# Three heads of k and w_phi's second copy on other DMA queues, zero matmuls in a bank of their own, and a new order

## The chip, the cores and the metric

The kernel runs on one core of a Trainium2 chip. The metric is the device time of one execution in microseconds (us), as the median of the runs. The engines are TensorE (PE, with its weight loads as PEld), VectorE (DVE), ScalarE (ACT), GpSimd (POOL) and SyncE (SP). SP issues DMAs only; ACT and POOL can issue them too. In this kernel POOL's loads cast fp32 to bf16 on the way; those of SP and ACT do not cast.

## The reference

Linear attention with a Hedgehog feature map over 8 batches, 8 heads, 576 positions and 64 dimensions, followed by a gated feed-forward network (FFN) on 4608 tokens:

```python
def phi(x):
    proj = np.einsum('bhsd,df->bhsf', x, w_phi)
    proj = proj - np.max(np.abs(proj), axis=-1, keepdims=True)
    return np.concatenate([np.exp(proj), np.exp(-proj)], axis=-1)
q_p, k_p = (phi(q), phi(k))
kv = np.einsum('bhsf,bhsd->bhfd', k_p, v)
z = np.sum(k_p, axis=2)
num = np.einsum('bhsf,bhfd->bhsd', q_p, kv)
den = np.einsum('bhsf,bhf->bhs', q_p, z)[..., None] + 1e-06
attn = num / den
...
x = attn.transpose(0, 2, 1, 3).reshape(B * S, H * D)
out = (np.maximum(x @ w_gate, 0.0) * (x @ w_val)) @ w_out
```

w_phi is 64 x 128, w_gate and w_val are 512 x 1536, w_out is 1536 x 512; all inputs are fp32.

## The kernel before

The whole program is one list of steps, ORDER, written out in full. Each word is one step: a two-letter name, its arguments, the PSUM banks after a colon, and after an @ the buffer of a ring that it takes. A loop at the end runs through the list and calls `do_<name>`, so ORDER sets the order of the instructions on every engine and every DMA queue; each engine runs its own steps in that order, and waits for semaphores in it.

Each batch goes through the same stages, and the FFN of earlier batches is laid between them:

- **Loads.** `lk`, `lq`, `lm`, `ln` (k, q and the last 64 positions of each) are cast to bf16 by POOL's queue, and so are the weights `wl` (w_val, w_gate) and `wo`. `lv` and `lw` (v) go over SP's queue, except for batch 0, where `lv` goes over POOL's. HEADS splits the eight heads into groups 0 (two heads), 1 and 2 (three each). `wp` and `wq` load two copies of w_phi over SP's queue: w32f, read four times into 32 rows, and w64f, read twice into 64 rows; `wc` and `wd` cast them to bf16 on DVE. `gt` is a small DMA on SP that reads k's group 0 of batch 0 and so holds SP's queue until that group has landed.
- **k of batch 0** (`k0`, `k1`, `k2`): PE transposes a group's k into a bank (`k0`), DVE copies it to kT (`k1`), and PE multiplies it by w64 into four banks (`k2`). The other batches transpose on DVE (`kt`, `ku`) and project with `kr`, which uses w32.
- **k's features**: `ke` are the exponentials on ACT (two signs for each of four banks), `kx` the row maxima of the magnitudes on DVE, `kk` and `kp` the exponentials of these maxima. `vs`, `vd`, `vr`, `vo`, `vp` scale v by them, on POOL and DVE.
- **q's features**: `qt` transposes on DVE, `qs` and `qc` project on PE with w32, `qe` are the exponentials on ACT, `qx` the maxima on DVE; `qy`, `qz`, `qu`, `qw` turn these into scales.
- **kv and the numerators**: `kv` on PE, copied out by `kc` (ACT) or `kd` (DVE); `nu` on PE, joined on DVE by `nt`, `nv` and `nr`, divided on POOL by `nx`.
- **FFN**: `xp`, `xa` and `xc` (or `xt`, a DMA) transpose the result, `pv`, `pg`, `fv`, `fg` project it, `va`, `vb`, `pa`, `pb`, `pc`, `ga` are copies and products on ACT and DVE, `fo` and `fp` the output projection, `oc` and `oe` its copies, `od` the store. `mt`, `mc`, `me`, `mx`, `mn` and others do the same for the last 64 positions of q.

`zz.N` are N matmuls of a zeroed tile into a bank that nobody reads; `zero` is filled by `ms.0`, and `ms` steps fill other constants. At the start PE's queue holds zz.37, k0.1, zz.5, k2.1, zz.6, k0.2, zz.7, k2.2, k0.0, zz.7, k2.0, then the eight `qs` of batch 0, `qy` and the three `kv`.

Of the kernel before, what the change touches and what calls it, by code (L numbers as in the profile page):

```python
# [34 lines left out]
nt.0.1.1:1@t2 qz.0.3:4@my0 nu.0.1.2:5 qw.0.2 nv.0.1.1:1@u1 lq.1.2 nt.0.1.2:5@t0 kr.1.1:7630
nx.0.0@xu0 ke.1.1.3.1:0@kp2 wl.1.1 ke.1.1.0.0:7 nu.0.1.0:2 nt.0.1.0:2@t2 nu.0.2.0:4 xp.0.0:1
xa.0.0:1 nv.0.1.2:5 nv.0.1.0:2 wo.0 nu.0.2.1:5 nr.0.1@r0 nx.0.1@xu0 kx.1.1.3:0@mk2 wl.0.2 nu.0.2.2:2
lm.2.0 nt.0.2.1:5@t2 ke.1.1.3.0:0 nt.0.2.2:2@t0 nt.0.2.0:4@t1 ke.1.1.1.1:6 lm.2.1 qu.0.3@mz0
kx.1.1.2:3 pv.1.0:1 pa.1.0:1@val0 ke.1.1.1.0:6 nv.0.2.0:4@u1 nv.0.2.1:5 nv.0.2.2:2 nr.0.2@r0
pg.0.0:0 nx.0.2@xu1 kx.1.1.0:7 kx.1.1.1:6 qw.0.3 xp.0.1:1 nu.0.3.1:4 xa.0.1:1 ke.1.1.0.1:7  # L40
ke.1.1.2.0:3 nt.0.3.1:4@t0 nv.0.3.1:4@u0 qt.1.1@qT0 pv.0.0:5 pa.0.0:5@val1 pv.0.1:1 pb.0.0:0
pg.0.1:7 kk.1.1.0@ek1 pa.0.1:1@val2 ke.1.1.2.1:3 lw.1.0 xp.0.2:5 xa.0.2:5 qc.1.1:1462
qe.1.1.3.1:2@qp2 qe.1.1.2.1:6@qp0 qe.1.1.0.0:1@qp1 pb.0.1:7 lv.1.3 lv.1.1 qx.1.1.1:4 qe.1.1.2.0:6
qe.1.1.0.1:1 nu.0.3.2:0 nt.0.3.2:0@t0 kt.1.0 nu.0.3.0:5 nv.0.3.2:0 nt.0.3.0:5@t2 pv.1.1:3
pa.1.1:3@val2 qe.1.1.1.1:4@qp3 qx.1.1.2:6 qx.1.1.0:1 kk.1.1.1 vo.1.1@vs2 qx.1.1.3:2 pv.0.2:7
nv.0.3.0:5 pa.0.2:7@val1 qe.1.1.3.0:2 pg.1.1:0 pb.1.1:0 nr.0.3@r0 ln.0.0 pg.0.2:6 pb.0.2:6 pg.1.0:1
qe.1.1.1.0:4 kr.1.0:2573 ke.1.0.1.1:5@kp0 ke.1.0.3.1:3 ke.1.0.2.1:7 ke.1.0.0.0:2 ke.1.0.3.0:3
pv.1.2:4 qt.1.0@qT0 kx.1.0.1:5@mk2 lw.1.1 pa.1.2:4@val1 ke.1.0.0.1:2 nx.0.3@xu1 xp.0.3:6 xc.0.3:6
kx.1.0.2:7 wl.1.2 pg.1.2:0 pb.1.0:1 ke.1.0.2.0:7 ke.1.0.1.0:5 kx.1.0.3:3 pv.0.3:6 pa.0.3:6@val0
fv.0.8:4 va.0.8:4@val2 ln.0.1 qc.1.0:5371 wo.2 pv.1.3:6 vs.1.1.0 kx.1.0.0:2 kk.1.0.0@ek0 kk.1.0.1  # L50
qe.1.0.1.1:3 vr.1.0.1 vs.1.0.0@vs0 pb.1.2:0 qx.1.0.2:7 qx.1.0.0:5 kt.1.2@kT1 qe.1.0.2.1:7
qe.1.0.3.0:1 qe.1.0.0.0:5 vr.1.1.0 qe.1.0.2.0:7 ms.1 pc.1.3:6@val1 pg.0.3:4 pb.0.3:4 qx.1.0.3:1
fv.0.10:0 va.0.10:0@val3 fv.0.11:2 lk.2.3 qe.1.0.0.1:5 va.0.11:2@val0 qx.1.0.1:3 kr.1.2:0476
kx.1.2.0:0@mk2 ke.1.2.3.0:6@kp1 pg.1.3:5 fg.0.11:2 kx.1.2.2:7 kx.1.2.3:6 qe.1.0.1.0:3 ke.1.2.1.1:4
kx.1.2.1:4 ke.1.2.2.0:7 qe.1.0.3.1:1 ku.2@kT1 ke.1.2.0.1:0 pb.1.3:5 kk.1.2.0@ek2 ke.1.2.2.1:7
fv.0.9:3 va.0.9:3@val1 fg.0.8:1 ke.1.2.1.0:4 wo.1 lv.2.3 ga.0.11:2 vr.1.0.0 qy.1.0:7 qz.1.0:7@my0
mt.0 fg.0.10:5 ga.0.8:1 kk.1.2.1 ke.1.2.0.0:0 vs.1.0.1 mc.0:4732 me.0.2.0:3 mx.0.3:2 me.0.0.0:4
qu.1.0@mz0 mx.0.2:3 me.0.0.1:4 vr.1.1.1 vo.1.0 kv.1.0:0 kc.1.0:0@kv1 ga.0.10:5 mx.0.0:4 qw.1.0@cq0
mx.0.1:7 vs.1.1.1 kv.1.1:1 me.0.2.1:3 kc.1.1:1 nu.1.1.0:0 nt.1.1.0:0@t2 fg.0.9:5 vo.1.2@vs1 lv.2.0
kt.2.1@kT0 vs.1.2.1 nu.1.0.0:1 me.0.3.1:2 ga.0.9:5 ke.1.2.3.1:6 nu.1.0.1:4 nu.1.1.1:3 nt.1.1.1:3@t0  # L60
nt.1.0.0:1@t1 vs.1.2.0 kv.1.2:6 nv.1.1.0:0@u0 nv.1.1.1:3 me.0.1.0:7 kt.2.0 lw.2.1 fo.0.1.0:5
kc.1.2:6 nu.1.0.2:6 nt.1.0.2:6@t0 nu.1.1.2:3 nt.1.0.1:4@t2 me.0.3.0:2 nu.1.2.0:2 nt.1.2.0:2@t3
nv.1.0.0:1@u1 me.0.1.1:7 lq.2.2 nv.1.0.2:6 nv.1.0.1:4 nr.1.0@r0 nv.1.2.0:2@u2 fo.0.1.1:5 fo.0.1.2:5
oc.0.1:5@ob0 nt.1.1.2:3@t2 nu.1.2.2:4 nt.1.2.2:4@t3 lw.2.0 nv.1.1.2:3 nr.1.1@r1 kr.2.0:2617
ke.2.0.0.0:2@kp0 kx.2.0.3:7@mk2 lv.2.1 ke.2.0.0.1:2 od.0.1 nu.1.2.1:0 nt.1.2.1:0@t2 nx.1.0@xu1
kx.2.0.2:1 ke.2.0.1.1:6 kx.2.0.0:2 nu.1.3.2:5 nt.1.3.2:5@t0 nv.1.2.1:0 ke.2.0.3.1:7 fo.0.0.0:3
fo.0.0.1:3 nv.1.3.2:5@u1 xt.1.0 fo.0.0.2:3 nu.1.3.0:5 ke.2.0.2.1:1 nv.1.2.2:4 nr.1.2@r0
nt.1.3.0:5@t3 nx.1.1@xu0 nu.1.3.1:0 nt.1.3.1:0@t0 nv.1.3.0:5 nv.1.3.1:0 nr.1.3@r1 ke.2.0.3.0:7
ke.2.0.2.0:1 oc.0.0:3@ob0 ke.2.0.1.0:6 kt.2.2@kT1 nx.1.2@xu2 kr.2.1:4172 ke.2.1.2.0:7@kp1 kx.2.0.1:6
fo.0.2.0:3 fo.0.2.1:3 ke.2.1.1.1:1 xt.1.1 ke.2.1.0.1:4 ke.2.1.3.1:2 fo.0.3.0:0 ke.2.1.0.0:4  # L70
# [996 lines left out]
```

## Time and profile before

| what | value |
|---|---|
| time, median of 3 runs | 378.46 us (378.4 to 378.5) |
| the profiled execution | 378.79 us, span 376.8 us |
| mean granted TensorE clock in it | 0.986 |
| PE busy | 367.3 us (97%) |
| DVE busy | 296.3 us (79%) |
| ACT busy | 222.6 us (59%) |
| POOL busy | 161.4 us (43%) |
| chain that ended last | PE 89%, DVE 5%, ACT 4%, DMA 2% |
| DMA | 38.04 MB in 90513 packets |

The page cuts the span into 40 slices of 9.4 us and prints a digit for the busy share of each (9 is 90% or more); PEclk is the clock that PE was granted, in tenths of full speed. The chain of waits goes back from the last instruction, at each step to what released it, and gives start, length and what. Windows give busy time in chosen stretches, with the number of instructions, the clock, the DMA share and the bytes moved. PE's busy time is that of pipelined matmuls with modelled ends, so PE can be busy without doing its best.

### The profile page before, as it was taken

To read this page: it belongs to the slowest core of one execution; us is meant where nothing else is said; L and a number is where in the kernel's file an instruction comes from. 1 tells how busy PE (TensorE), PEld (TensorE's weight loads), DVE (VectorE), ACT (ScalarE), POOL (GpSimd) and SP (SyncE) were. 2 spreads that over 40 slices of the span, in tenths; PEclk is the share of its full clock that TensorE was granted. 3 is DMA by queue.
4 is the path that set the end of the run, shared out by engine and by line. 5 is a ranking of instruction groups with operands and counts; after the bars stand their busy time and mean duration, and the time that the engine had idled before them with its cause. 6 is when DMAs were issued, how large, how long until landed. Compare 5 with 4: busy or idle time off the path is not lost.

```text
span 376.8 us, 9181 instructions
## 1 busy us (share of the span) xinstructions
PE 367.3 (97%) x3591; PEld 197.2 (52%) x3591; DVE 296.3 (79%) x680; ACT 222.6 (59%) x539; POOL 161.4 (43%) x180
## 2 busy tenths in 40 slices
PE   8788999999999999999999999999999999999996
...
PEclk9859999999999999999999999999999999999999
...
DMA packets 90513, 38.04 MB, mean 101 GB/s; under 512 B 64230, under 2 KB 85734, under 8 KB 90470
## 3 DMA queue, kind: packets, MB, share of 16 engines
...
q10 hardware_dynamic: 144, 0.13, 0.1%
...
## 4 chain that ended last, share of the span: by engine, by line
PE 89%; DVE 5%; ACT 4%; DMA 2%; issue 0%; SPq 0%; DVEq 0%; ACTq 0%
PE bank L916 46%; PE bank L977 22%; PE bank L658 6%; PE bank L757 4%; PE bank L945 4%; PE bank L694 3%; ACT kp L563 2%; PE bank L511 2%; DMA w64f<-in_w_phi_dram 2%; DVE mk L571 1%; ACT qp L709 1%; PE bank L1006 1%; PE bank L898 1%; DVE u L788 1%; DVE maxq L717 1%; DVE t L778 1%
## 5 line engine op out<-in xcount | busy, mean ns | idle before, releaser
L563 ACT ACTIVATE kp<-bank 128x384 bf16<-128x384 f32 x192 | 83.2, 513 | 26.2 <-PE bank L511 15.0
L977 PE MATMUL bank<-wo,h 128*128 128x512 bf16 x420 | 98.3, 379 | 0.0
L937 DVE SCALAR_TENSOR_TENSOR h<-bank,val 128x512 bf16<-128x512 f32 x100 | 66.3, 681 | 29.8 <-PE bank L916 25.5
L916 PE MATMUL bank<-xTs,wg 128*128 128x512 bf16 x352 | 86.7, 379 | 0.0
L916 PE MATMUL bank<-xTs,wv 128*128 128x512 bf16 x352 | 86.2, 379 | 0.0
L800 POOL TENSOR_TENSOR xu<-u,r 128x512 bf16<-128x512 f32 x36 | 37.5, 1044 | 97.3 <-DVE r L796 92.4
L931 ACT CAST val<-bank 128x512 bf16<-128x512 f32 x70 | 41.6, 606 | 62.2 <-PE bank L916 50.8
L709 ACT ACTIVATE qp<-bank 128x512 bf16<-128x512 f32 x128 | 70.9, 632 | 10.1 <-DVE maxq L717 5.1
L618 POOL TENSOR_TENSOR vs<-vn,ek 128x780 bf16<-128x780 f32 (+3 forms) x40 | 53.0, 1338 | 37.8 <-ACT ek L580 35.1
L977 PEld LDWEIGHTS <-h 128*128 128x128 bf16 x420 | 39.1, 98 | 44.0 <-issue 0.9
L916 PEld LDWEIGHTS <-wv 128*128 128x128 bf16 x400 | 37.0, 98 | 43.2 <-issue 3.5
L916 PEld LDWEIGHTS <-wg 128*128 128x128 bf16 x400 | 37.4, 98 | 42.0 <-issue 1.8
L571 DVE TENSOR_REDUCE mk<-bank 128x3 f32<-128x384 f32 x96 | 49.0, 539 | 4.3 <-ACT kp L563 2.2
L717 DVE TRANSPOSE_TENSOR_REDUCE maxq<-bank 128x16 f32<-128x512 f32 x64 | 42.3, 692 | 3.5 <-PE bank L694 2.3
L986 ACT COPY ob<-bank 128x512 f32<-128x512 f32 x23 | 13.6, 593 | 37.5 <-PE bank L977 37.2
L788 DVE TENSOR_TENSOR u<-bank,t 128x195 f32<-128x195 f32 (+1 forms) x108 | 33.4, 330 | 1.9
L778 DVE TENSOR_TENSOR t<-bank,cq 128x195 f32<-128x195 f32 (+1 forms) x96 | 29.8, 327 | 5.0 <-PE bank L757 4.1
L757 PEld LDWEIGHTS <-qp 128*128 128x128 bf16 x512 | 24.1, 98 | 13.6 <-issue 2.0
L757 PE MATMUL bank<-kv,qp 128*128 128x65 bf16 x512 | 27.2, 194 | 1.2 <-ACT qp L709 0.8
L934 DVE CAST val<-bank 128x512 bf16<-128x512 f32 x30 | 20.2, 678 | 8.4 <-PE bank L916 8.3
L658 PEld LDWEIGHTS <-kp 128*128 128x128 bf16 x640 | 24.0, 101 | 3.7 <-DVE h L937 0.3
L658 PE MATMUL bank<-vs,kp 128*128 128x65 bf16 x512 | 24.2, 199 | 0.0
...
## 6 DMA issues: line engine op xcount, KB each, us to landing
...
```

The costliest lines, as they stand in the source:

```text
L563: nc.scalar.activation(kp_of(3 * b + j)[:, i, s].rearrange("p n f -> p (n f)"), bank[bk[0]][:, 0 : 3 * F], AF.Exp, scale=(1.0, -1.0)[s],)
L571: nc.vector.tensor_reduce(mk_of(3 * b + j)[:, :, i], bank[bk[0]][:, 0 : 3 * F].rearrange("p (n f) -> p n f", f=F), axis=AX.X, op=ALU.max, ...
L618: nc.gpsimd.tensor_tensor(vs_of(3 * b + j)[:, s, 0:n].rearrange("p n i e -> p (n i) e")[:, :, 0:e], src[:, lo:hi].rearrange("p h i e -> p ...
L658: nc.tensor.matmul(out_ps[:, h - lo, s, :], lhsT=lhsT, rhs=rhs, start=(at == 0), stop=(at == 2 * n * (C + 1) - 1),)
L709: nc.scalar.activation(qp_of(4 * b + i)[:, s, 4 * hq : 4 * hq + 4].rearrange("p h m -> p (h m)"), bank[bk[0]], AF.Exp, scale=(1.0, -1.0)[s],)
L717: nc.vector.tensor_reduce(maxq[:, :, i, 4 * hq : 4 * hq + 4].rearrange("p t h -> p h t"), bank[bk[0]].rearrange("p (h t u) -> p h t u", h= ...
L757: nc.tensor.matmul(bank[bk[0]][:, E * n : E * (n + 1)], lhsT=qp_of(4 * b + i)[:, s, h, :], rhs=kv_of(b)[:, h, s, :],)
L800: eng.tensor_tensor(xu_of(n).rearrange("p (h d) -> p h d", d=D), u_of(n)[:, :, 0:D], r_of(n).to_broadcast([P, H, D]), op=ALU.mult,)
L916: nc.tensor.matmul(bank[bk[0]], lhsT=w[:, dc, P * f : P * f + P], rhs=xT(g)[:, dc, :], start=(dc == 0), stop=(dc == NDC - 1),)
L931: nc.scalar.copy(val_of(NFC * g + f), bank[bk[0]])
L937: nc.vector.scalar_tensor_tensor(h2_of(g, f), bank[bk[0]], 0.0, val_of(NFC * g + f), op0=ALU.max, op1=ALU.mult)
L977: nc.tensor.matmul(bank[bk[0]], lhsT=h2_of(g, f)[:, P * t : P * t + P], rhs=wo_sb[:, f, :], start=(f == 0), stop=(f == NFC - 1),)
```

## The change

The list ORDER is replaced as a whole; its steps are the same but for these:

- `lk.0.1`, k's group 1 of batch 0 by POOL's queue with the cast, is replaced by `lf`: the same three heads as fp32 over SP's queue, into xT_mix, whose own use comes late. `cg.1` (ACT, one head) and `cf.0` (DVE, two heads) cast them into kn.
- `wq` is replaced by `wr`, the same load over ACT's queue, now the first step of ACT. `wp` moves from SP's first place to behind `gt.0`, and `wc` and `if` (a copy of the identity) move into DVE's work behind `k1`.
- The zero matmuls of the start are 78 in twelve places instead of 62 in five, and from the second group on all go to bank 1, which no other step uses before qy.0.1, ahead of the last two of them. New are those between k0.0 and k2.0, between k2.0 and the first qs, and among the qs.
- On POOL `lk.0.2` and `lk.0.0` come ahead of `lq.0.1`, and `wl.1.0` comes behind all vs of batch 0.
- Later in the list, copies out of PSUM change engines: `kd` (DVE) goes from 5 to 2 and `kc` (ACT) from 19 to 22; `va`, `vb`, `pa`, `pc`, `oc`, `oe` change by one or two each.

The order is shown to the first numerator of batch 0's second block:

```diff
--- before
+++ after
 ORDER = """
-ms.0 ms.2 ms.3@vr0 lk.0.1 ms.6 wp wq ms.4@vr1 wd ms.5 lq.0.1 wc id if zz.37:0 k0.1:0 k1.1:0@kT0
-zz.5:1 k2.1:0123 lk.0.2 ke.0.1.1.0:1@kp0 ke.0.1.2.0:2 ke.0.1.3.0:3 ke.0.1.0.0:0 qt.0.1@qT0
-ke.0.1.3.1:3 kx.0.1.1:1@mk0 lk.0.0 kx.0.1.2:2 ke.0.1.2.1:2 ke.0.1.1.1:1 lm.0.1 zz.6:4 k0.2:4
-k1.2:4@kT0 zz.7:5 k2.2:4567 ke.0.2.2.0:6@kp1 kx.0.1.3:3 ke.0.2.3.1:7 lm.0.0 lq.0.0 kx.0.1.0:0
-kx.0.2.0:4@mk1 ke.0.1.0.1:0 lw.0.0 k0.0:2 k1.0:2@kT0 zz.7:1 k2.0:2013 kk.0.1.1@ek0 ke.0.2.1.1:5
-qt.0.0@qT1 kx.0.2.3:7 ke.0.2.2.1:6 kx.0.2.2:6 kx.0.0.0:2@mk2 lv.0.1 ke.0.0.2.1:1@kp2 ke.0.2.1.0:5
-lm.1.0 lv.0.0 ke.0.0.3.1:3 ke.0.0.1.0:0 ke.0.2.0.0:4 lv.0.2 ke.0.0.0.1:2 kk.0.1.0 lm.1.1 wl.1.0
-kx.0.2.1:5 kp.0.2.1:7 ke.0.0.0.0:2 ke.0.2.0.1:4 lw.0.1 qs.0.1.0:6 kx.0.0.1:0 kx.0.0.3:3 qx.0.1.0:6
-vs.0.1.1@vs0 kp.0.2.0:7 qs.0.0.1:5 qe.0.0.1.0:5@qp0 gt.0 lk.1.3 qs.0.0.2:2 lv.1.2 kx.0.0.2:1
-ke.0.2.3.0:7 vp.2:7@vs1 kk.0.0.1@ek1 vs.0.1.0 ke.0.0.2.0:1 qs.0.0.0:4 wl.0.1 kk.0.0.0 ke.0.0.3.0:3
-qx.0.0.0:4 qx.0.0.2:2 vo.0@vs2 vd.0.2.0:7 ke.0.0.1.1:0 qs.0.1.1:1 qe.0.0.1.1:5 qe.0.0.0.1:4@qp1
-qx.0.1.1:1 qs.0.1.2:3 qe.0.1.2.0:3@qp2 qe.0.0.0.0:4 qs.0.0.3:0 qe.0.0.3.0:0@qp3 wl.0.0 qe.0.1.0.0:6
-qs.0.1.3:4 qx.0.0.1:5 qe.0.0.3.1:0 vd.0.2.1:7 qe.0.1.0.1:6 qe.0.1.1.0:1 vr.0.0.0 vr.0.0.1 qy.0.0:5
-qx.0.1.2:3 vr.0.1.0 qx.0.1.3:4 vr.0.1.1 kv.0.2:7 kc.0.2:7@kv0 vo.1 kv.0.1:6 qz.0.0:5@my0 qu.0.0@mz0
-qw.0.0@cq0 qx.0.0.3:0 kt.1.1@kT0 nu.0.0.2:7 nt.0.0.2:7@t0 qe.0.1.3.1:4 qy.0.1:0 qz.0.1:0@my0
-vs.0.0.1 kc.0.1:6 ku.1@kT1 vs.0.0.0 kv.0.0:5 qe.0.1.3.0:4 nu.0.0.1:6 nt.0.0.1:6@t1 kc.0.0:5
-qe.0.0.2.0:2 qu.0.1@mz0 qw.0.1 qy.0.2:0 qe.0.1.1.1:1 nv.0.0.1:6@u0 qe.0.1.2.1:3 qy.0.3:4 nu.0.0.0:5
-nt.0.0.0:5@t2 qe.0.0.2.1:2 nv.0.0.2:7 nv.0.0.0:5 nr.0.0@r0 nu.0.1.1:1
-...
+ms.0 ms.3@vr0 ms.4@vr1 wr lf ms.5 cg.1 ms.2 lk.0.2 id lk.0.0 cf.0 wd zz.16:0 k0.1:0 ms.6 k1.1:0@kT0
+zz.3:1 k2.1:0234 kx.0.1.1:2@mk0 k0.2:5 ke.0.1.3.1:4@kp0 kx.0.1.3:4 k1.2:5@kT0 ke.0.1.2.0:3 lq.0.1
+kx.0.1.0:0 if ke.0.1.1.1:2 ke.0.1.3.0:4 ke.0.1.2.1:3 ke.0.1.1.0:2 zz.7:1 k2.2:5674 kx.0.1.2:3
+ke.0.2.2.1:7@kp1 ke.0.2.0.0:5 kx.0.2.1:6@mk1 ke.0.1.0.0:0 lm.0.0 ke.0.2.3.1:4 kx.0.2.2:7
+ke.0.2.1.0:6 ke.0.1.0.1:0 ke.0.2.1.1:6 lm.0.1 kx.0.2.0:5 zz.4:1 k0.0:3 k1.0:3@kT0 lw.0.1 kx.0.2.3:4
+qt.0.1@qT0 ke.0.2.2.0:7 ke.0.2.0.1:5 kk.0.1.1@ek0 lv.0.1 zz.12:1 k2.0:3206 lq.0.0 qt.0.0@qT1
+ke.0.0.3.1:6@kp2 ke.0.0.0.1:3 gt.0 lm.1.1 ke.0.0.2.0:0 wp wc kx.0.0.3:6@mk2 kp.0.2.1:4 kp.0.2.0:4
+zz.10:1 qs.0.0.1:5 ke.0.0.0.0:3 kx.0.0.2:0 ke.0.0.3.0:6 kx.0.0.1:2 qe.0.0.1.0:5@qp0 kk.0.1.0
+qs.0.1.0:7 lv.0.2 ke.0.0.2.1:0 ke.0.0.1.0:2 kx.0.0.0:3 kk.0.0.1@ek1 lv.0.0 vd.0.2.1:4@vs0
+ke.0.0.1.1:2 lk.1.3 qe.0.1.0.1:7@qp1 qx.0.0.1:5 lw.0.0 vd.0.2.0:4 zz.2:1 qs.0.1.1:6 kk.0.0.0 zz.3:1
+qs.0.0.0:3 qe.0.0.0.0:3 qs.0.0.3:0 vs.0.1.1@vs1 ke.0.2.3.0:4 lv.1.2 qe.0.1.1.1:6 qx.0.1.0:7 lm.1.0
+wl.0.1 qe.0.0.1.1:5 qe.0.0.0.1:3 vs.0.1.0 zz.2:1 qs.0.0.2:2 qx.0.0.2:2 qx.0.1.1:6 qe.0.1.0.0:7
+zz.13:1 qs.0.1.2:5 vp.2:4 qe.0.0.2.0:2@qp2 qe.0.1.2.1:5 qe.0.0.2.1:2 zz.4:1 qs.0.1.3:7 qx.0.0.0:3
+qy.0.0:3 vr.0.0.0 kt.1.1@kT0 ku.1@kT1 vr.0.1.1 vr.0.1.0 wl.0.0 vr.0.0.1 kv.0.2:4 qe.0.1.3.1:7@qp3
+qz.0.0:3@my0 qx.0.1.2:5 vs.0.0.1@vs2 qe.0.0.3.0:0 qx.0.1.3:7 kc.0.2:4@kv0 vo.1 qu.0.0@mz0 kv.0.1:3
+kc.0.1:3 qx.0.0.3:0 vo.0 nu.0.0.2:4 qw.0.0@cq0 nt.0.0.2:4@t0 vs.0.0.0 kv.0.0:2 kc.0.0:2 nu.0.0.1:3
+ms.1 nv.0.0.2:4@u0 nt.0.0.1:3@t1 lv.1.0 qe.0.0.3.1:0 qy.0.1:1 qz.0.1:1@my0 qu.0.1@mz0 wl.1.0
+qe.0.1.1.0:6 qy.0.3:2 qe.0.1.3.0:7 lq.1.2 nu.0.0.0:4 nt.0.0.0:4@t0 nv.0.0.1:3 qw.0.1 nv.0.0.0:4
+nr.0.0@r0 qy.0.2:0 qz.0.2:0@my0 qz.0.3:2@my1 zz.2:1 nu.0.1.1:6
+...
 """
```

The rest of the diff; `HEADS[1]` is (2, 5), and `lf`, `cf`, `cg` and `wr` are called by the loop over ORDER:

```diff
@@ -378,6 +379,9 @@
     def do_wq(bk):
         nc.sync.dma_start(out=w64f, in_=w_phi[None].to_broadcast([2, D, F]))
 
+    def do_wr(bk):
+        nc.scalar.dma_start(out=w64f, in_=w_phi[None].to_broadcast([2, D, F]))
+
     def do_wc(bk):
         nc.vector.tensor_copy(w32.rearrange("p a f -> p (a f)"), w32f.rearrange("p a f -> p (a f)"))
 
@@ -418,6 +422,31 @@
             out=kn_of(b)[:, lo:hi],
             in_=k[b, lo:hi, 0:SF, :].rearrange("h (p c) d -> p h c d", c=C),
         )
+
+    def k_first():
+        flat = xT_mix.rearrange("p a b -> p (a b)").bitcast(FP32)[:, 0 : 3 * C * D]
+        return flat.rearrange("p (h x) -> p h x", h=3)
+
+    def do_lf(bk):
+        lo, hi = HEADS[1]
+        nc.sync.dma_start(
+            out=k_first().rearrange("p h (c d) -> p h c d", d=D),
+            in_=k[0, lo:hi, 0:SF, :].rearrange("h (p c) d -> p h c d", c=C),
+        )
+
+    def cast_first(copy, half):
+        lo, hi = ((0, 2), (2, 3))[half]
+        at = HEADS[1][0]
+        copy(
+            kn_of(0)[:, at + lo : at + hi].rearrange("p h c d -> p h (c d)"),
+            k_first()[:, lo:hi],
+        )
+
+    def do_cf(bk, half):
+        cast_first(nc.vector.tensor_copy, half)
+
+    def do_cg(bk, half):
+        cast_first(nc.scalar.copy, half)
 
     def do_lq(bk, b, hq):
         lo, hi = (4 * hq, 4 * hq + 4) if hq < 2 else (0, H)
```

More of the change, by code (lines that the diff above doesn't have):

```diff
@@ L35 @@
[L35 to L70, printed above, removed]
@@ new lines @@
+fo.2.2.2:1 ke.4.1.2.1:2 ke.4.1.1.0:7 lm.5.1 oc.2.2:1@ob1 kr.4.2:5260 ke.4.2.1.0:2@kp0 vr.4.0.0
+ke.4.2.2.0:6 ke.4.2.3.0:0 kx.4.1.1:7 kk.4.1.0@ek2 mn.1.2:7 nt.3.3.0:3@t1 nv.3.3.0:3 od.2.2
+oe.2.0:4@ob2 mn.1.0:4 mn.1.1:1 nr.3.3@r2 nx.3.3@xu2 kk.4.1.1 xt.3.3 kx.4.2.0:5@mk0 od.2.0
+nt.8.1.0:4@t1 nv.8.1.0:4@u1 nt.8.1.1:1@t2 nv.8.1.1:1 nt.8.1.2:7@t1 nv.8.1.2:7 ke.4.2.0.1:5
+fo.2.1.0:3 fo.2.1.1:3 ke.4.2.3.1:0 vs.4.0.0@vs1 fo.2.1.2:3 kx.4.2.3:0 qt.4.1@qT1 ke.4.2.2.1:6
+vs.4.1.1@vs0 ke.4.2.1.1:2 ke.4.2.0.0:5 qc.4.0:0714 qe.4.0.0.0:0@qp1 fo.2.3.0:5 qe.4.0.2.1:1@qp2
```

404 lines of the change are left out of this document (217 added, 187 removed).

## Prediction

> **What bounds the kernel now.** I read the page's 40 slices first. They show where TensorE (PE) is not full and where its clock was cut.
>
> ```profile
> PE   8788999999999999999999999999999999999996
> ...
> PEclk9859999999999999999999999999999999999999
> ```
>
> Only the first three slices (28 us) hold gaps, and the clock is cut in slices 2 and 3. Next, busy time by stage:
>
> ```profile
> 40.00:60.00 20.00, 20.00 (x320) 14.55 (x318) 19.79 (x44) 19.45 (x51) 16.98 (x21) 1.00 1.20 165
> ...
> 340.00:360.00 20.00, 20.00 (x94) 9.11 (x93) 6.08 (x10) 4.01 (x7) 0.00 (x0) 1.00 0.11 27
> ```
>
> From 32 us to the end PE has work in every stretch. In the timeline, the starts of its matmuls there lie as close as they can (216 ns for 512 columns); what exceeds that, beside 95 ns at each change to row-tiled matmuls, sums to about 0.5 us. Whatever the change does before 32 us therefore moves the end by the same amount, and nothing later has much to give. The chain of waits up to there (start, length, what):
>
> ```profile
> 1.56 6.35 DMA w64f<-in_w_phi_dram
> ...
> 7.94 0.23 DVE w L385
> 8.16 0.14 DVE maxq L400
> 8.30 0.27 DVE w L382
> 8.57 0.13 DVE identf L391
> 8.70 0.48 DVE kT L536
> ...
> 9.23 0.47 PE bank L554 x11
> ...
> 9.72 3.95 ACT kp L563 x10
> ...
> 23.50 3.30 PE bank L658 x60
> ...
> 31.77 0.55 PE bank L757 x12
> ```
>
> Two things are seen. The first exponential (step ke, ScalarE, ACT) starts at 9.72 because the 64-row copy of w_phi lands at 7.91 and five VectorE (DVE) steps stand between it and the first projection (k2.1). After 9.72 ACT and DVE are nearly full until 31.8: of 22 us ACT idles 1.3 and DVE 1.7. The kv matmuls (L658) are in the chain at 55 ns each, where the next 20, from 27.2, take 32 ns. The windows say why (columns: PE, PEld, DVE, ACT, POOL, clock, DMA share, GB/s):
>
> ```profile
> 9.73:13.14 3.41, 3.24 (x44) 2.50 (x43) 3.40 (x7) 3.41 (x9) 2.91 (x4) 1.00 1.23 270
> 13.14:16.55 3.41, 1.59 (x20) 0.70 (x19) 3.41 (x8) 3.41 (x11) 1.53 (x2) 1.00 1.04 228
> 16.55:19.97 3.42, 2.98 (x9) 0.59 (x10) 3.11 (x7) 3.42 (x14) 3.38 (x5) 0.50 1.21 195
> 23.38:26.79 3.41, 3.41 (x65) 3.41 (x64) 3.05 (x6) 2.17 (x6) 2.92 (x4) 0.50 1.23 203
> ```
>
> PE was busy 1.59 of 3.41 us from 13.14, and the clock was 0.50 from 16.55 to 26.79. It returned after a stretch filled with kv.
>
> **The change, part by part.** Call a the start of the first exponential; it is 9.72 now.
>
> *Landing of w64f (wr).* In the trace's packet records its 128 packets run on two DMA engines, 64 on each, from 4.59 to 7.50, behind the packets of w32f from the same queue. On one engine they start 77 ns apart beside POOL's packets (60 ns each) and 30 ns apart when alone. The new order starts it at the head of ACT's queue, so first packets come near 2.27, as w32f's do now; wp moves behind gt.0. But lf puts 24 packets of 1 KB (46 ns, as w32f's) on each of the 16 engines at the same moment, and lk.0.2 comes behind. Middle: 2.27, 0.4 of slow first packets (as now), 24 rounds with lf at 80 ns (1.9), 24 beside lk.0.2 at 77 (1.85), 16 alone at 30 (0.5), 0.4 from last packet to landing: 7.3. Lower end, 64 packets at 30 ns: 5.0. Upper end, all three in turn for 24 rounds (125 ns) and then pairs (77): 9.1. I take 7.3, the case built from the pairings that the trace shows.
>
> The Trainium skill (DMA: Bandwidth & Descriptors, Rules for kernel authors) speaks against the step: spreading DMAs over queues does not add bandwidth, since all run on the same 16 engines, and a leading broadcast of two copies confines a DMA to two of them. The trace agrees with the second half (two trains of 64). Going by the rule alone, wr would save its issue time only.
>
> *Steps behind it.* Now wd 0.23, ms.5 0.14, wc 0.27, if 0.13, k1.1 0.48; afterwards wd, ms.6 (as ms.5), k1.1, so 0.40 less. k2.1 then runs at half clock, since the zeros of now start 213 ns apart until 6.15 and 109 ns after, so that zz.16 ends near 4.5, still at 213, and leaves PE idle: its six pairs take 56 ns more each, 0.28. So a = 7.3 + 0.02 + 0.23 + 0.14 + 0.48 + 0.05 + 0.47 + 0.02 + 0.28 = 9.0: a gain of 0.7.
>
> *lf, cg.1, cf.0.* lf lands near 5.2: its 24 packets share two engines with w64f until 4.75. The casts wait for it. cf.0 is at the head of DVE with wd and k1.1 behind it; 512 columns at 1 ns each (L385 and L382: 0.227 and 0.353 for 128 and 256) are 0.6. cg.1 stands before all of ACT's work and takes 0.4 while ACT is idle anyway. k0.1 then ends by 6.6, and k1.1 could end at 7.1. That is before 8.2, where w64f allows it, so all this is hidden. If w64f came at once, this chain would set a: 7.1 + 0.05 + 0.75 = 7.9.
>
> *wp behind gt.0.* gt.0 holds SyncE until lk.0.0 lands (near 7.5, as POOL's queue is one DMA ahead of now), so wp is issued near 9 and lands after 4.7 to 6.5 us (mark and lv.1.2 now): 13.3 to 15.5. wc waits for it with kx.0.0.*, vd and qx queued behind, and all qs wait for wc. DVE gets there only after k1.1, eight kx, two k1, if and two qt, at a + 7.5 = 16.5. Hidden by 1 to 3 us. lw.0.0 and lv.1.* follow wp and are wanted later.
>
> *DVE from a.* Increments in the timeline: kx 0.463, k1 0.463, qt 1.03, qx 0.60, vd 0.843, wc 0.27, if 0.13, kt 0.75. In the new order 12 kx, 2 k1, if, 2 qt, wc, 2 vd, 8 qx, vp, kt, ku, qz and qu stand before the first nt: 16.9, with 0.5 of waits for k2.2 and k0.0: a + 17.4. Now the first nt starts at 27.15, a + 17.43. DVE takes on 0.8 (wc, if and 0.32 of qt.0.1, which run before a now, and ku), and gives up 0.8 of the 1.3 that it idles there now, mostly behind slow PE work. From there to the last nv before 31.9 the work is the same but ku (0.22, already done) and ms.1 (0.085, new): 0.1 less.
>
> *ACT from a.* The same 24 ke, 16 qe, kk, kp and kc. It reaches kc.0.2 at a + 16.0 with two qe more before it than now, and ends kc.0.0 at a + 18.2 (now 18.5).
>
> *Zero matmuls and clock.* 78 instead of 62, the added ones ahead of k2.0 and between the qs. At 109 ns zz.12 is 1.3 and zz.13 1.4, inside PE's waits for DVE and ACT. With full clock the 80 kv matmuls take 23 ns less each: 1.8, of which only what ACT and DVE waited counts; DVE's share went above, ACT's leaves it idle less. So the clock's gain is spent mostly on the steps that DVE took on.
>
> *The rest of the order.* The same matmuls, tail and number of row-tiled groups. A few copies change between ACT and DVE (three kd become kc, two va and one oc go), 0.1 to 1 us over 345 us. As PE now lost 0.5 to waits there, I take 0, bounds -0.3 and +1.
>
> Sum: -0.7 - 0.1 = -0.8. The profiled execution took 378.79 (span 376.8 and 2.0 around it), 0.33 over the median of 378.46; applied to the median: 377.6.
>
> **Rivals.**
> *Queue of its own helps fully.* w64f is served at 30 to 45 ns a packet and lands by 6; k's chain sets a at 7.9, which gives 378.46 - 1.8 - 0.1 = 376.6. For it: w32f's packets ran 47 ns apart while POOL's waited. Against: lf starts on the same engines at the same time.
> *Clock stays at half (slower).* Zero matmuls at 213 ns are a cost in PE's queue: zz.7, k2.2, zz.4, k0.0 and zz.12 then end at a + 6.9, k2.0 at a + 7.5, where ACT wants it at a + 6.3: +1.2. If the clock falls again between the qs, kv.0.2 to kv.0.0 end 1.6 later and 1.2 of it stays: 378.8 with one, 380.0 with both. It decides when the stretch of 3.4 us after k2.1 does not lift the clock. For it: 2.98 of 3.42 us busy with 32-row qs did not lift it now. Against: 7 + 4 + 12 full-array zeros fill that stretch. The Trainium skill (TensorE: Matmul & The Clock Gate, Why this matters for your kernels) asks only that no PE gap exceed about 3 us, by which there is no fall in either kernel; this trace differs, with no gap over 1.4 us before the fall at 16.55.
> *w64f gets later.* With fair turns among three queues, or behind ACT's table load (1.28 us, first on ACT now), it lands at 9; a is 10.4 or more, 379.1. The Trainium skill's rule on queues, cited above, points this way.
> *The new order stalls later.* Beyond 32 us ACT and DVE are at 97% and more up to 60; a misjudged wait there costs up to 1: 378.6.
>
> **How the numbers follow.** Forecast 0.40 (its own range 377.1 to 378.1), queue 0.22, half clock 0.14 for one loss and 0.08 for both, later landing 0.10, later stalls 0.06. 0.2% (0.76 us) is about what a measurement can tell from no change. Faster by more means below 377.70: half of the forecast and nearly all of the queue case, 0.42. Slower means above 379.22: half clock twice and parts of three others, 0.20. Between: 0.38. The range runs from the queue case less 1.0 (lf and w64f both sooner) to between one and two clock losses.
>
> **What would show it.** Right: w64f lands at 7 to 7.6 and DVE's wd ends its longest wait there; first kp exponential at 8.8 to 9.2; clock 1.00 from about 13 on; kv at 32 ns; PE without gaps from about 31. Wrong: the first exponential near 8 or past 10; clock 0.50 beyond 16.5; ACT idle before L563 of k2.0; or an early shift that is missing at the end.

## The result, and the profile after

The changed kernel takes 383.53 us (median of 6 runs, 381.5 to 385.86), the kernel before on the same chip 378.43 (6 runs, 378.36 to 379.1): ratio 1.0133, 95% interval 1.0096 to 1.017. It is slower by 5.1 us, far outside 0.2%, and outside the range of the prediction. The profiled run took 383.2, its span is 381.4. (In all results below the ratio leaves out runs that lie far above the fastest of the same kernel, so it can be a little under the quotient of the medians.)

The page's slices after:

```profile
PE   7699999999999999999999999999999999999996
...
PEclk9959999999999999999999999999999999999999
```

At the front, two of the 40 slices are under 9 (four were before), but the half clock lies later: in the third slice instead of the second and third. Stages of 20 us, in the columns PE, PEld, DVE, ACT, POOL, clock, DMA share, GB/s:

```profile
40.00:60.00 20.00, 20.00 (x300) 14.89 (x300) 19.26 (x38) 18.85 (x47) 14.26 (x19) 1.00 0.97 142
...
340.00:360.00 20.00, 20.00 (x94) 9.04 (x93) 7.14 (x11) 2.73 (x5) 0.00 (x0) 1.00 0.00 0
```

So PE is still full from 40 us on, and most of the loss must be made before. The chain of waits (start, length, what) names the place:

```profile
2.70 4.59 DMA kn<-in_k_dram
...
7.31 0.62 SPq L495
...
7.98 8.14 DMA w32f<-in_w_phi_dram
...
16.14 0.39 DVE w L386
...
16.58 0.63 PE bank L723 x4
...
20.85 2.88 PE bank L412 x13
...
27.02 2.82 PE bank L687 x60
```

The chain no longer goes through w64f and the first exponential, but through lk.0.0, gt.0 (L495) and w32f, which gt.0 holds back: issued at 7.98, it lands at 16.12. Behind it, in the chain, stand zero matmuls (L412) at 222 ns each (zz.13: 2.88 us) and the kv matmuls at 47 ns. The windows, over the same stretches as in the prediction, show what happened to the clock (same columns):

```profile
13.14:16.55 3.41, 0.51 (x5) 0.21 (x3) 1.01 (x3) 1.50 (x6) 3.25 (x4) 1.00 1.15 225
16.55:19.97 3.42, 3.36 (x18) 0.99 (x19) 3.42 (x7) 2.95 (x10) 1.47 (x1) 0.83 1.29 183
19.97:23.38 3.41, 3.41 (x15) 1.79 (x13) 3.29 (x6) 3.02 (x7) 3.26 (x6) 0.50 1.20 203
23.38:26.79 3.41, 3.41 (x11) 0.89 (x10) 1.00 (x3) 1.58 (x4) 3.41 (x6) 0.50 1.18 201
```

From the timeline, what each engine waited for in this hole (start, length, engine, line, operation; in brackets the idle time before it and what ended that):

```profile
16.14 0.38 DVE L386 CAST w<-w32f 128x256 bf16<-128x256 f32 x1 [2.40 <-DMA w32f<-in_w_phi_dram]
16.58 0.63 PE L723 MATMUL bank<-qT,w 32*128 32x512 bf16 x4 [2.93 <-DVE w L386]
17.02 0.49 ACT L592 ACTIVATE kp<-bank 128x384 bf16<-128x384 f32 x1 [2.35 <-DVE mk L600]
```

DVE waits 2.40 us for w32f, and PE, behind it, 2.93. From 13.14 to 16.55 PE is busy 0.51 of 3.41 us, DVE 1.01 and ACT 1.50; the clock falls at 18.82 and stays at 0.50 until 29.06. From 16.55 PE is busy throughout, but with zeros and 32-row qs at half speed, and ACT (1.58) and DVE (1.00) wait for it in the last row.

Four points in time tell where the difference comes from (us from the span's start; "fill" is the run after_fill below):

| | first exponential | first nt | first pv | first fo | end of span |
|---|---|---|---|---|---|
| before | 9.72 | 27.15 | 32.2 | 61.0 | 376.8 |
| after | 6.88 | 30.5 | 35.2 | 64.3 | 381.4 |
| fill | 7.22 | 26.8 | 31.5 | 60.6 | 378.0 |

The first exponential starts 2.84 us earlier, more than any rival of the prediction had; by the first pv (L974, the first FFN matmul) the kernel is 3.0 late, so 5.8 us are lost between the two. Another 1.6 goes between the first pv and the end.

### The profile page after: what moved, and what is told of

Its sections match the earlier page's. It is cut to its first block, busy times and chain, and to the rows that moved or that the text cites. A ratio compares the mean times of both kernels' runs of the same rounds, so it can differ in the third digit from the quotient of the medians.

```text
span 381.4 us, 9227 instructions
## 1 busy us (share of the span) xinstructions
PE 371.2 (97%) x3607; PEld 198.2 (52%) x3607; DVE 297.0 (78%) x680; ACT 223.2 (59%) x541; POOL 160.1 (42%) x179
## 3 DMA queue, kind: packets, MB, share of 16 engines
HBM read 37.95 MB, written 9.44 MB: 124 GB/s over the span
## 4 chain that ended last, share of the span: by engine, by line
PE 79%; issue 8%; DMA 4%; POOL 4%; DVE 3%; ACT 1%; SPq 1%; POOLq 0%; DVEq 0%
PE bank L945 39%; PE bank L1006 19%; PE bank L687 4%; PE bank L974 4%; PE bank L723 3%; PE bank L786 3%; DMA w32f<-in_w_phi_dram 2%; PE bank L540 2%; POOL xu L829 2%; PE bank L412 1%; DMA kn<-in_k_dram 1%; DMA vn<-in_v_dram 1%; POOL vr L666 1%; PE bank L1035 1%; DVE t L807 1%
## 5 line engine op out<-in xcount | busy, mean ns | idle before, releaser
L592 ACT ACTIVATE kp<-bank 128x384 bf16<-128x384 f32 x192 | 81.4, 515 | 19.0 <-PE bank L540 10.0
L960 ACT CAST val<-bank 128x512 bf16<-128x512 f32 x68 | 39.9, 599 | 82.1 <-PE bank L945 70.7
L817 DVE TENSOR_TENSOR u<-bank,t 128x195 f32<-128x195 f32 (+1 forms) x108 | 34.6, 332 | 3.0 <-POOL xu L829 0.8
L963 DVE CAST val<-bank 128x512 bf16<-128x512 f32 x32 | 21.7, 680 | 8.5 <-PE bank L945 8.0
L666 POOL TENSOR_TENSOR vr<-vm,ek 64x260 bf16<-64x260 f32 x32 | 19.6, 617 | 12.4 <-ACT ek L609 10.0
L687 PEld LDWEIGHTS <-kp 128*128 128x128 bf16 x640 | 23.1, 100 | 3.2 <-ACT val L960 0.6
```

The lines of the kernel that those rows point to most:

```text
L592: nc.scalar.activation(kp_of(3 * b + j)[:, i, s].rearrange("p n f -> p (n f)"), bank[bk[0]][:, 0 : 3 * F], AF.Exp, scale=(1.0, -1.0)[s],)
L687: nc.tensor.matmul(out_ps[:, h - lo, s, :], lhsT=lhsT, rhs=rhs, start=(at == 0), stop=(at == 2 * n * (C + 1) - 1),)
L960: nc.scalar.copy(val_of(NFC * g + f), bank[bk[0]])
```

## The experiments

The kernel before ran beside every set of runs: its medians were 379.36, 379.13, 378.93, 379.27 and 379.41 us in the five sets. Each ratio is to the kernel before in the same set.

**1. w32f early, and no zeros among the qs.** Theory W: the late w32f. Theory Z: the zeros at half clock.

wp_early:
```
-ms.0 ms.3@vr0 ms.4@vr1 wr lf ms.5 ... ke.0.0.2.0:0 wp wc
+ms.0 ms.3@vr0 ms.4@vr1 wr lf wp ms.5 ... ke.0.0.2.0:0 wc
```


> One step moved: wp (w_phi's 32-row copy) goes right behind lf in SyncE's queue, ahead of gt.0. Theory W (the late w32f is the loss: DVE stood 2.4 us in front of wc, PE idled 2.9 us, and the clock fell after that): w32f lands near 6 to 7, wc waits for nothing, the first exponential stays near 7 to 7.5, PE's gap ahead of the first qs goes, and the clock holds in most runs; 376.0 to 377.5 us. Rival Z (the zero matmuls among the qs are the loss by themselves, as they hold kv in PE's queue): kv.0.2 still begins 17 us or more after the first exponential, 380 us or more.

nozz, and wp_early_nozz (both edits):
```
-zz.2:1 qs.0.1.1:6 kk.0.0.0 zz.3:1 qs.0.0.0:3
+qs.0.1.1:6 kk.0.0.0 qs.0.0.0:3
...  (all 24 zeros between the first qs and qy.0.0)
```


> The changed kernel without the 24 zero matmuls between the first qs and qy.0.0 (zz.2, zz.3, zz.2, zz.13, zz.4). Theory W: w32f still lands near 16, the clock still falls, but 24 times 213 ns leave PE's queue, of which about half was waited for by ACT and DVE: 380.5 to 382 us, still slower than before by 2 or more. Rival Z: with the zeros gone the early start comes through, 378 us or less.

> Both edits: wp right behind lf, and none of the 24 zeros among the qs. Theory W: within 0.7 us of the kernel with wp moved alone (376 to 378), kv perhaps at half clock as before the change. Rival Z: clearly the best of the three, and below the one with wp moved alone by 2 us or more.

Measured: wp_early 380.61 (379.34 to 384.17), ratio 1.0054 (1.0022 to 1.0086); nozz 380.86 (380.7 to 381.53), 1.0037 (1.0025 to 1.0049); both 381.84 (379.6 to 382.34), 1.0037 (1.0013 to 1.0061). They are 0.4 to 0.5% over before, where the changed kernel was 1.3% over: each edit takes back more than half of the loss, and both together take back no more than one. Neither theory is whole. In wp_early wc no longer waits for w32f, but w32f's 128 packets on four DMA engines now stand in the way of k's third group, kn.0.2, which lands at 8.53 instead of 6.63, and ScalarE loses 2 us there:

```profile
11.68 2.79 ACT L592 ACTIVATE kp<-bank 128x384 bf16<-128x384 f32 x7 [2.00 <-PE bank L583]
```

(L583 is k2.2.) PE still waits 1.38 us for wc in wp_early, since the cast itself takes 1.54 us where it took 0.38 in the changed kernel. GpSimd runs vs.0.1.1 at that moment:

```profile
15.94 1.54 DVE L386 CAST w<-w32f 128x256 bf16<-128x256 f32 x1
15.83 1.49 POOL L647 TENSOR_TENSOR vs<-vn,ek 128x768 bf16<-128x768 f32 x1
```

The cast ends 0.16 us behind that step. With both edits it takes 1.23 and again ends 0.16 behind it; in the run spread below, with GpSimd idle, it takes 0.28. How one engine holds the other up is not shown. In nozz the wait of wc stays (2.06) and the clock falls all the same, from 18.42 to 28.66.

**2. The queue for w64f alone.** before_wr: `wq` becomes `wr` in the order of before.


> The kernel before with one step of the change alone: w64f's load on ScalarE's queue (wr in the place of wq). w64f lands near 5 to 5.5 instead of 7.9 if a queue of its own serves it as in the changed kernel; the first exponential is then bound by zz.37 and k0.1 (8.0) and comes near 9.2 instead of 9.7: 377.9 us (377.6 to 378.2). If the queue brings nothing, 378.4.


Measured: 378.83 (378.41 to 379.72), ratio 0.9984 (0.997 to 0.9998); first exponential 9.44 instead of 9.72. w64f lets wd start at 5.95 instead of 7.94, but then TensorE waits for k's first group, which GpSimd loads here, until 7.78. So the queue alone is worth 0.3 at the first exponential; the 2.84 of the change need lf too.

**3. Both copies spread; the parts in the old order; two spliced orders.** In spread and its relatives, w32f is right behind lf and each copy is several transfers:

```
-out=w32f.rearrange("p a f -> p (a f)"),
-in_=w_phi.rearrange("(r a) f -> r (a f)", a=2)[None].to_broadcast([4, R, 2 * F]),
+for i in range(4):                       # four transfers
+    out=w32f[R * i : R * (i + 1)].rearrange("p a f -> p (a f)"),
+    in_=w_phi.rearrange("(r a) f -> r (a f)", a=2),
-out=w64f, in_=w_phi[None].to_broadcast([2, D, F])
+for i in range(2):                       # two transfers
+    out=w64f[D * i : D * (i + 1)], in_=w_phi
```


> The changed kernel with both copies of w_phi spread: w32f in four transfers of 32 rows right behind lf on SyncE, w64f in two transfers of 64 rows on ScalarE's queue, so that neither is confined to 4 or 2 DMA engines. Theory 'confined copies': the 2.4 us wait of wc goes, kn.0.2 lands before 7 and not at 8.5, ScalarE has no idle stretch over 0.5 us before 20, the clock stays at 1.00 from 14 on; the time is the changed kernel's less 3.2 (lost before 40 us): 380.3, or, with the gain of 2.8 at the first exponential kept, 377.5. Rival 'zeros and clock': the clock falls to 0.50 all the same, because the zeros and the 32-row qs do not hold it, and the zeros between the qs take 213 ns: 381 or more.

Measured: 378.91 (377.07 to 383.36), ratio 0.9987 (0.9959 to 1.0015). kn.0.2 lands at 7.04 and not at 8.53, w32f's last part at 6.70, w64f at 4.66, and no wait of wc is left. So it was the copies on few engines that held kn.0.2 back in wp_early. The Trainium skill (DMA: Bandwidth & Descriptors, Rules for kernel authors) asks for this: an outermost dimension that is a multiple of 16, since a leading broadcast of c copies confines the transfer to c engines; the 1.5 us between the two landings of kn.0.2 are its price in these two traces (both copies were spread at once). Yet the runs lie far apart, and they go with the clock: six at 1.00 have spans of 375.3 to 376.3, three at 0.991 to 0.995 have 377.9 to 378.4, three at 0.98 and 0.982 have 380.4 to 381.6. A window of 3.41 us at half clock lowers a run's mean clock by 0.0045. By the runs such a window costs 1.5 us in the changed kernel (379.7 at 0.991, 384.1 at 0.978) and 1.0 to 1.4 in this one (medians of 375.8 at 1.00, 378.2 at 0.991 and 381.4 at 0.982; 380.4 at 0.98), but 0.7 in before (medians of 376.6 at 0.991 and 378.0 at 0.982, all sets together), which has no zeros between the qs. The profiled run (0.991), whose clock falls at 22.71, shows where the engines wait now; that these waits pull the clock down is not shown. In its timelines GpSimd idles 5.18 us ahead of lk.1.3, and a kv matmul waits for GpSimd later:

```profile
14.41 0.91 POOL L423 DMA_DIRECT2D kn<-in_k_dram  x1 [5.18 <-ACT kp L594]
```
```profile
23.09 0.21 PE L689 MATMUL bank<-vr,kp 128*128 128x65 bf16 x1 [0.78 <-POOL vr L668]
```

The releaser in the first line is not to be believed: that exponential does not touch kn. lk.1.3 overwrites kn, which the mark of gt.0 still reads, and the mark lands at 13.84, 0.57 ahead of lk.1.3; in the changed kernel and in after_fill the same 0.57 us lie between the two. In before, vs.0.1.1 stood ahead of lk.1.3 and used such a wait.

parts_spread is the order of before with lf, cg.1, cf.0, wr and wp at its head, zz.16 for zz.37, and qt.0.1 behind k1.0:
```
-ms.0 ms.2 ms.3@vr0 lk.0.1 ms.6 wp wq ms.4@vr1 wd ms.5 lq.0.1 wc id if zz.37:0 k0.1:0 k1.1:0@kT0
+ms.0 ms.2 ms.3@vr0 wr lf wp lk.0.2 id lk.0.0 lq.0.1 cg.1 cf.0 ms.6 ms.4@vr1 wd ms.5 zz.16:0
+k0.1:0 k1.1:0@kT0 wc if
```


> The parts without the new order: the order of before, with k's first three heads in fp32 and cast, w64f on ScalarE's queue and w32f behind lf, both spread as in the run spread, zz.37 cut to zz.16, and the first transpose of q moved behind k1.0. Theory 'the parts are sound, the order spends them': the first exponential is at about 7 (before: 9.7) and 2 to 2.7 of it arrive at the end: 375.8 to 376.5. Rival 'the start of the exponentials is not what bounds the early part' (the loads of k, q and v land when they land): under 0.7 arrives, 377.8 or more.


Measured: 377.84 (377.17 to 379.18), ratio 0.9968 (0.9955 to 0.998); first exponential 6.95, and of these 2.8 us 1.2 arrive. The clock is at 0.50 from 14 to 24 here too, but in this order no zeros stand between the qs.

late_new and spread_late_old splice two orders at the first kr of the second batch:
```
late_new:        before ... nx.0.0 ... | kr.1.1 ... of after
spread_late_old: spread ...           | kr.1.1 ... of before
```


> The kernel before up to the first kr of the second batch (about 33 us), then the changed kernel's order from there to the end: prices the later part of the new order alone. Theory 'new order loses later': what the changed kernel lost between 40 us and the last matmul (1.1) and behind the last matmul (0.36) is lost here too: 378.4 + 1.5 = 379.9. Rival 'the later losses follow from the early ones': 378.4, with 3.1 us behind the last matmul or not more than 0.4 over before.

> The run spread up to the first kr of the second batch, then the order of before from there to the end. Theory 'confined copies' with 'new order loses later': 1.5 less than the run spread, 376 to 378.8 as that run comes out. Rival 'the later losses follow from the early ones': the same time as the run spread within 0.4.


Measured: late_new 383.23 (382.46 to 384.21), ratio 1.0105 (1.0086 to 1.0124); spread_late_old 380.61 (379.49 to 384.22), 1.0048 (1.0023 to 1.0074). Neither prices the later order, since a splice changes the queues as well. In late_new SyncE issues four loads of the second batch's v by 17.2 (two in before), the FFN weights land over 3 us later (30.09 and 33.13 against 26.55 and 29.89), and all six runs have a clock of 0.978 to 0.982. In spread_late_old the clock is 1.00 in the profiled run (0.978 to 1.00 in all), but the weights come in the order of one half and are used in that of the other, and PE waits 1.3 us for wg. These two are misses.

**4. Late but spread, GpSimd's step, and zeros in the old order.**
late_spread: the changed kernel with w32f's four transfers where `wp` stands in it, w64f as it is.


> The changed kernel with w32f left behind gt.0 where the change put it, but loaded in four transfers of 32 rows instead of one that is confined to 4 DMA engines; w64f stays as it is. Theory 'confined copy': the first packets come as late as before (12.6, 4 us behind the issue), but the 128 packets then take 0.7 and not 2.9 us, the last part lands by 14.3, wc waits 0.5 at most instead of 2.4, ScalarE's idle time of 2.35 shrinks under 0.7, the clock does not fall at 18.8, and the time is that of the run spread plus at most 1: 379 to 380. Rival 'too late whatever its shape': with four issues on SyncE and landings of 5 us and more behind each, the last part lands at 16 or later and the time stays at 383.


Measured: 382.41 (378.82 to 384.56), ratio 1.0078 (1.005 to 1.0106). I had blamed the four engines for most of the wait; that fell. The four parts land from 13.52 to 15.45, the last 0.67 us ahead of the one transfer, and wc still waits 1.7 us. At this place the copy is late in both shapes: its packets run from 10.07 to 14.52 among those of v.

spread_pool and spread_pool_nozz:
```
-... lk.1.3 ... vs.0.1.1@vs1 ... wl.0.1 ... wl.0.0 ... vs.0.0.0
+... vs.0.1.1@vs1 lk.1.3 ... wl.0.0 ... vs.0.0.0 wl.0.1
```


> The run spread with three GpSimd steps moved: vs.0.1.1 ahead of lk.1.3 (which holds GpSimd from 9.2 to 14.4 until the mark's transfer has read kn), wl.0.0 at the place of wl.0.1, and wl.0.1 behind vs.0.0.0. Theory 'GpSimd is the next bound' (in the run spread kv.0.2 waits for vr until 23.1 and for vs until 24.3, TensorE falls under half busy at 20 to 23.4 and the clock goes to 0.50 from 23): vr and vs end 2.3 earlier, kv runs at 32 ns, the first nt comes 2 us sooner, 376.9. Rival 'something else ends last': under 0.5 arrives, 378.4 or more.

> The run spread_pool without the 24 zero matmuls among the qs. Theory 'zeros hold the clock where no wait interrupts them': without them the clock falls to 0.50 between 16 and 24, kv takes 55 ns a matmul, and the time is 1 to 2 us over the run spread_pool. Rival 'zeros are only in the way': the same or up to 0.5 faster.


Measured: 378.35 (377.49 to 380.81), ratio 0.9998 (0.9975 to 1.002), and 378.2 (377.57 to 379.65), 0.9977 (0.9963 to 0.999). At full clock the first pv comes at 29.4, 2.8 before that of the kernel before; but three of 12 runs are at 0.986 (spans of 379.0), and after the first pv PE waits 0.6 for a transpose of the second batch's q, which lands at 34.87. My next theory put this down to the moved weights. That does not hold: spread_vs_fill below leaves the weights in place and waits as long for the same q (landed 35.18), while spread_vs just escapes it (34.47). In these orders, with the first pv before 30, that load is what PE meets next. Without the 24 zeros every run loses clock (0.982 to 0.991), and the median is the same: the zeros pay for themselves when they hold the clock, and cost as much when they don't.

parts2 (old order, with the new zeros in free banks, and ms.4 moved as in parts3 below):
```
-zz.7:1 k2.0:2013 ... qs.0.1.0:6 ... qs.0.0.1:5 ... qs.0.0.2:2
+zz.12:1 k2.0:2013 ... zz.10:6 qs.0.1.0:6 ... zz.3:5 qs.0.0.1:5 ... zz.3:2 qs.0.0.2:2
...
```


> The run parts_spread (the old order with the parts of the change) with the memset of vr 1 moved from ahead of wd to the first steps, and the new order's zeros put in the same places of the old order (12 for 7 ahead of k2.0, 4 ahead of k0.0, 37 among the qs, on banks that are free), to hold the clock that falls there from 14 to 24. Theory 'the clock is worth what kv and the qs lose at half speed': the clock stays at 1.00, kv takes 32 ns, 1.0 to 1.9 less than the run parts_spread, 376 to 376.8. Rival 'zeros sit in TensorE's queue ahead of qs that ScalarE and VectorE wait for': as much is lost as gained, 377.5 to 378.5.


Measured: 378.94 (378.24 to 380.48), ratio 0.9993 (0.9981 to 1.0006). All 12 runs are at 0.995 or more, and yet it is 1.1 slower than parts_spread, and 1.3 to 1.4 slower than parts3, from which it differs by the zeros alone: kv starts at 23.35 instead of 21.49, because the zeros stand in PE's queue ahead of qs that ACT and DVE wait for. The rival was right here: full clock alone is not worth the zeros.

**5. The wait or the clock.** after_fill leaves the changed kernel as it is, w32f late, and fills the hole:
```
-zz.10:1 qs.0.0.1:5
+zz.36:1 qs.0.0.1:5
```


> The changed kernel with zz.10 ahead of the first qs made zz.36: 26 more zero matmuls, 2.8 us at 109 ns, in the 2.93 us in which TensorE waits for wc; nothing else is changed, w32f lands as late as it does. Theory 'the clock takes more than the wait': the clock stays at 1.00 beyond 18.8 in most runs, the zeros between the qs take 109 ns and kv 32 ns, and what stays is the wait alone: 379 to 380.5, 3 to 4.5 less than the changed kernel. Rival 'the wait is the loss': 382.5 to 384, as the changed kernel, with kv at 32 ns all the same. If the clock falls although the hole is filled, the time is that of the changed kernel too, but then the windows show 0.50.


Measured: 379.7 (378.96 to 380.52), ratio 1.001 (0.9998 to 1.0023). All 11 runs have a clock of 0.999 or 1.00. DVE still waits 2.0 us for w32f. The windows of its trace (same columns and stretches as above):

```profile
13.14:16.55 3.41, 3.41 (x33) 3.05 (x32) 1.36 (x4) 1.84 (x7) 3.32 (x4) 1.00 1.04 208
16.55:19.97 3.42, 3.42 (x22) 0.89 (x19) 3.42 (x7) 3.03 (x10) 2.01 (x2) 1.00 1.33 198
19.97:23.38 3.41, 2.82 (x21) 1.73 (x21) 3.29 (x7) 3.11 (x7) 3.25 (x6) 1.00 1.23 198
23.38:26.79 3.41, 3.41 (x87) 2.92 (x87) 3.21 (x9) 3.22 (x8) 3.41 (x6) 1.00 1.16 188
```

In the first row DVE and ACT idle as before (1.36 and 1.84 busy), only PE is full; in the last, PE does 87 matmuls where the changed kernel did 11. Of the 5.1 us, twenty-six useless matmuls take back 3.8 by the medians and 4.7 by the ratios to before, which itself was 0.8 slower in this set. The runs of late_spread say the same without any edit between them: w32f is late in that kernel too, and its two runs at full clock took 378.82 and 379.24, its three at 0.982 383.65 to 383.84. That settles it: the wait of 2.4 us is paid for by the earlier start, and the clock that falls behind it makes the loss.

**6. What the early start can bring.** spread_vs moves one step of spread; spread_vs_nozz also drops the 24 zeros:
```
-... lk.1.3 ... vs.0.1.1@vs1
+... vs.0.1.1@vs1 lk.1.3 ...
```


> The run spread with vs.0.1.1 moved ahead of lk.1.3 and nothing else (the order of the weights as the change has it). Theory 'GpSimd is the next bound, and the weights moved in spread_pool cost 0.7 between the first pv and the first fv': kv.0.2 ends 1.5 sooner than in the run spread, the first pv comes at 30 to 30.5, and a run with the clock at 1.00 has a span of 375.0 to 375.3 (spread 375.3 to 376.3, spread_pool 375.7 to 376.1); the median, over runs with and without half clock, 377.3 to 378.3. Rival: spans at full clock as in the run spread.

> The run spread_vs without the 24 zero matmuls among the qs. Theory 'without zeros the clock falls in every run, but costs little': the clock is 0.982 to 0.991 in every run, the runs lie within 1.5, and the median is 377.3 to 378, no higher than that of spread_vs. Rival 'the zeros are worth their place': 0.5 or more above the median of spread_vs.


Measured: spread_vs 378.54 (376.56 to 382.04), ratio 0.9994 (0.9969 to 1.002): nine of 12 runs are at 0.995 or more with spans of 374.8 to 377.6, three at 0.982 to 0.986 with 379.0 to 380.3; first pv at 29.8. spread_vs_nozz 377.92 (377.66 to 378.65), 0.9973 (0.9962 to 0.9984), all nine runs at 0.985 to 0.991, as its theory said.

parts3, from parts_spread:
```
-ms.0 ms.2 ms.3@vr0 ... cf.0 ms.6 ms.4@vr1 wd
+ms.0 ms.2 ms.3@vr0 ms.4@vr1 ... cf.0 ms.6 wd
```


> The run parts_spread with the memset of vr 1 (0.93 on VectorE, just ahead of wd) moved to the first steps, without further zeros. Theory 'start of the exponentials': it starts at 6.3 to 6.5 instead of 6.95, and 0.4 of it arrives: 377.4. Rival 'the old order has its bound elsewhere (banks that wait for kx)': 377.8 as before.


Measured: 377.58 (377.24 to 377.78), ratio 0.9959 (0.9946 to 0.9972). The first exponential is at 6.21 instead of 6.95; 0.3 of that arrives.

spread_vs_fill puts zeros into the two holes that are left:
```
-zz.10:1 qs.0.0.1:5 ... zz.13:1 qs.0.1.2:5
+zz.18:1 qs.0.0.1:5 ... zz.19:1 qs.0.1.2:5
```


> The run spread_vs with 14 more zeros in the two holes that TensorE has left there: zz.18 for zz.10 ahead of the first qs (0.94 us of waiting for wc) and zz.19 for zz.13 ahead of qs.0.1.2 (0.77 us of waiting for ScalarE). Theory 'TensorE's fill decides the clock': no run shows a clock under 0.995, the spans are those of the full-clock runs of spread_vs (374.8 to 377.6), the median 377 to 377.8 and the spread of the runs under 2. Rival 'the clock falls for another reason too': some runs at 0.982 to 0.986 again with spans of 379 and more, median as spread_vs, 378.5.


Measured: 377.74 (376.54 to 378.38) against 379.41, ratio 0.9953 (0.9935 to 0.9971); six runs at 0.999 or 1.00, 1.8 us apart instead of 5.5. The windows of its trace are full where those of the changed kernel stood still:

```profile
13.14:16.55 3.41, 3.41 (x26) 1.46 (x24) 3.41 (x8) 3.21 (x12) 3.39 (x5) 1.00 1.10 215
16.55:19.97 3.42, 3.42 (x27) 2.11 (x25) 3.42 (x7) 3.17 (x8) 3.36 (x5) 1.00 1.29 175
```

This and parts3 beat both kernels by most: by their ratios, 1.8 us (0.5%) and 1.6 us (0.4%) under before; their intervals overlap.

## Why the prediction was wrong, step by step

**Landing of w64f (7.3 expected).** It landed at 5.47. Its 64 packets on each of two engines ran from 3.42 to 5.06, 24 ns apart for the most part and so without taking turns with anything: lf's last packet had started at 3.49, and lk.0.2 did not interleave as POOL's packets did in before. My pairings of 80 and 77 ns came from that trace and did not hold (and a packet alone took 24 ns there too, not the 30 that I used). The own-queue rival had the landing right (by 6). In before_wr the queue alone brought w64f in at 5.92 instead of 7.91, more than the 0.8 by which it was issued sooner.

**The k chain (a = 7.9 in that rival).** The first exponential was at 6.88, as lf landed at 3.90 and not near 5.2, and the two casts ended by 4.5.

**wp behind gt.0 ("hidden by 1 to 3 us").** This is the step that failed: the landing was not hidden, and DVE waited 2.40 us for w32f, PE 2.93. Three terms were off. DVE reached wc at 13.74 = a + 6.86 (I had a + 7.5), a itself was 2.1 sooner than 9.0, and w32f took 8.14 us from issue to landing where I took 4.7 to 6.5 from the mark and lv.1.2. The third was partly made up by the issue, which came at 7.98 and not near 9, so the landing moved only from 15.5 at most to 16.12. (The lower end should have been 13.7, 9 and 4.7, and not 13.3.) With DVE at 16.5, as forecast, the cover would still have held by 0.4. The first two terms took it away. The numbers for that stood in the text: in the rival with a = 7.9, DVE is at wc at 15.4 and the landing's upper end is 15.5, so the cover was gone there. I gave that rival 376.6 and 0.22 without working the cover out again for it.

**Half clock (the slower rival, 0.22 in all).** The mechanism was right: zeros at 213 ns in PE's queue, kv at half speed, and the signs named for it (0.50 beyond 16.5, the early shift missing at the end) are in the trace. Its place and its size were not. I let the 3.4 us after k2.1 decide, and full-array zeros did hold the clock there; it fell behind the hole at wc. And I priced it at 1.2 to 2.4, where after_fill measures 3.8 or more of the 5.1 us. The two rivals that I kept apart were one case: the earlier start makes the wait, the wait makes the hole, the hole takes the clock.

**DVE and ACT from a.** In after_fill, at full clock, the first nt comes at a + 19.6 with 2.0 of waiting for wc in it, so 17.6 without: I had 17.4. This sum was good, though its qt of 1.03 is 0.95 in the trace of before.

**The rest of the order (0, bounds -0.3 and +1).** In the first reading, PE's row (8788 at the front) has four slices under 9 and not three; its gaps go on to 32 us, where the windows put them too, so the sum did not hang on it. Between the first pv and the end the changed kernel loses 1.6 to before, after_fill 1.9. But parts3, in the old order, loses 1.0 there, and before_wr none. The tail behind the last matmul is 3.49 instead of 3.13. How much of the rest belongs to the new order, and how much to work that comes earlier than its loads, stays open; the spliced orders that were to tell it did not.
